# First product of two-slot expert units with the weights stationary, in a routed three-stage kernel

## Chip, cores and metric

One core of one Trainium2 chip runs the whole program. The metric is device microseconds of one launch; the median of three runs of the kernel before is 823.82 (823.65 to 824.0).

## What is computed

Attention over four batches of eight heads with window masks gives a matrix x of 2304 tokens by 512. Then come a feed-forward layer and a layer of eight experts in which each token goes to one expert:

```
h = x @ w_in                      # 512 x 2048
r = np.maximum(h, 0.0)
x = (s * (r * r) + b) @ w_out     # 2048 x 512
...
logits = xn @ en.T / tau          # both normalized, 8 experts
expert_idx = np.argmax(logits, axis=1)
gate_w = softmax(logits)[np.arange(N), expert_idx]
for e in range(E):
    mask = expert_idx == e
    h = np.maximum(x[mask] @ w1[e], 0.0)           # 512 x 1024
    out[mask] = gate_w[mask, None] * (h @ w2[e])   # 1024 x 512
```

## The kernel before

Every fp32 product is made of three products of a shorter type: each operand is split into a high part (a cast, on ACT) and a low part (what the cast left, a subtraction), and `mm3` (L271) adds high by high (L273), high by low (L274) and low by high (L275). The first operand is the stationary one (128 x 128, loaded by a weight load of its own), the second moves past it.

Attention and the feed-forward layer run first, interleaved. The tokens are sorted by expert into slots of 128. A unit is one or two slots of one expert. The first two slots (0, 1) belong to the most popular expert and are started early, while the feed-forward layer ends; the next two (2, 3) use the same weights, and then come a unit of two slots (4, 5) and five times a unit of one and a unit of two: 6; 7, 8; 9; 10, 11; and so on to 18; 19, 20. That is 21 slots, eight pairs and five singles; a tail for more slots stands in a branch that these inputs do not take.

For each unit `load` (L774) brings eight raw tiles of 512 KB by SP's queue, four of w1 and four of w2, and `split` (L789) makes the high parts on ACT (L802) and the low parts on DVE or, for one tile of four, on POOL (L803, L804). The parts go to one of two sets of buffers (`wp0`, `wp1`), which alternate by unit, so that a w1 tile of the unit after next can be split when this unit's first product has read it for the last time.

For each slot `gather` (L807) fetches 128 tokens by an indirect DMA of POOL. `xt` transposes them on PE into the bank px (four transposes, L818) and splits them into xh and xl. `g1` is the first product: the tokens are stationary, w1 moves, 48 matmuls of 512 columns in two halves, and ACT's relu gives h (L835). `ht` transposes h in eight blocks into two banks pt (L847) and splits them into hh and hl (L848, L849). `g2` is the second product, 24 matmuls of 512 columns with hh and hl stationary; DVE scales its rows by the gate into o (L860), and POOL scatters o by an indirect DMA (L861).

The banks px and pt, and those of the routing tables, come from one ring of three (`psT`, tag "tr"); `ph`, the first product's, from a ring of three, `po` from a ring of two. xh, xl, hh and hl have two buffers each, h has one, and the gathered tokens x have four.

PE runs in the order in which the program is written. The loop `slots` (L936) gives it: first product of slot j, transposes of the tokens of slot j + 1, second product of slot j - 1, transposes of h of slot j. The order on DVE, ACT, POOL and SP is set by the scheduler of the framework from the dependences, so one line of the program can stand far from its neighbour there. Ahead of the loop L911 to L934 write out the order of the first two slots, with the routing tables (`route_rest`, L675, `units`, L743, `slot_table`, L592) between them; DVE's arithmetic for the table and PE's matmuls into the bank ptabr (L611) give the gathers of all later slots.

Of the kernel before, what the change touches and what calls it, by code (L numbers as in the profile page):

```python
# [7 lines left out]
F32 = mybir.dt.float32  # L8
# [11 lines left out]
NTAIL = 7  # L20
# [27 lines left out]
class Kern:  # L48
# [740 lines left out]
    def split(self, j, after=None):  # L789
# [6 lines left out]
        for a in range(2):  # L796
            with ExitStack() as st:
                for ins in after[a] if after else ():
                    st.enter_context(self.tc.issue_after(ins.ins))
                for i in range(4):  # L800
                    h, l, r = w[8 * a + i], w[8 * a + 4 + i], self.raw[4 * a + i]
                    nc.scalar.copy(h, r)  # L802
                    eng = nc.gpsimd if i == 3 else nc.vector  # L803
                    eng.tensor_sub(l, r, h.bitcast(F32))  # L804
        return [w[4 * i:4 * i + 4] for i in range(4)]

    def gather(self, j, rows=NT):  # L807
        nc = self.nc
        x = self.xp.tile([P, DM], F32, tag="x", name=f"x{j}", bufs=4)
# [4 lines left out]
    def xt(self, j, x):  # L814
        nc = self.nc
        px = self.psT.tile([P, 512], F32, tag="tr", name=f"px{j}", bufs=3)
        for i in range(4):
            nc.tensor.transpose(px[:, P * i:P * i + P], x[:, P * i:P * i + P], self.ident)  # L818
        xh = self.xp.tile([P, DM], F32R, tag="xh", name=f"xh{j}", bufs=2)
        xl = self.xp.tile([P, DM], F32R, tag="xl", name=f"xl{j}", bufs=2)  # L820
        nc.scalar.copy(xh, px)
        self.last_xl = nc.vector.tensor_sub(xl, px, xh.bitcast(F32))
        return xh, xl

    def g1(self, j, xh, xl, w):
        nc = self.nc
        hs = self.pad.tile([P, EF], F32, tag="h", name=f"h{j}", bufs=1)

        def part(n):
            ph = self.psE.tile([P, 512], F32, tag="h", name=f"ph{j}_{n}", bufs=3)  # L830
            fs = slice(512 * n, 512 * n + 512)
            for k in range(4):
                ks = slice(P * k, P * k + P)
                self.mm3(ph, xh[:, ks], xl[:, ks], w[0][k][:, fs], w[1][k][:, fs], k == 0, k == 3)
            nc.scalar.activation(hs[:, fs], ph, AF.Relu)  # L835
        return hs, part

    def ht(self, j, hs):
        nc = self.nc
        hh = self.hp.tile([P, EF], F32R, tag="hh", name=f"hh{j}", bufs=2)  # L840
        hl = self.hp.tile([P, EF], F32R, tag="hl", name=f"hl{j}", bufs=2)
        for n in range(2):
            pt = self.psT.tile([P, 512], F32, tag="tr", name=f"pt{j}_{n}", bufs=3)
            fs = slice(512 * n, 512 * n + 512)
# [3 lines left out]
            nc.scalar.copy(hh[:, fs], pt)  # L848
            nc.vector.tensor_sub(hl[:, fs], pt, hh[:, fs].bitcast(F32))  # L849
        return hh, hl  # L850

    def g2(self, j, hh, hl, w):
        nc = self.nc
        po = self.psE.tile([P, 512], F32, tag="o", name=f"po{j}", bufs=2)
        for k in range(8):
            ks = slice(P * k, P * k + P)
            fs = slice(512 * (k % 2), 512 * (k % 2) + 512)
            self.mm3(po, hh[:, ks], hl[:, ks], w[2][k // 2][:, fs], w[3][k // 2][:, fs], k == 0, k == 7)
# [5 lines left out]
    def experts_early(self):  # L864
        self.gidx, self.sidx, self.gate, self.xs, self.xts = {}, {}, {}, {}, {}
# [15 lines left out]
    def experts_early3(self):  # L881
        self.xts[0] = self.xt(0, self.xs[0])
# [4 lines left out]
    def experts(self):  # L887
        nc, tc = self.nc, self.tc
        w, xs, xts, hts = self.w, self.xs, self.xts, {}
# [10 lines left out]
        first = {}  # L900
        for j, (u, _) in enumerate(slot):
            first.setdefault(u, j)
        n = len(slot)
        nstat = n - NTAIL
# [6 lines left out]
        hs0, part0 = self.g1(0, *xts.pop(0), w[0])  # L911
        part0(0)
        dots = self.logits_pe(NG - 1)
        part0(1)
        dots()
        tables = self.route_rest()
        xts[1] = self.xt(1, xs.pop(1))
        hts[0] = self.ht(0, hs0)
        hs1, part1 = self.g1(1, *xts.pop(1), w[0])
        part1(0)  # L920
        tables = tables()
        part1(1)
        hts[1] = self.ht(1, hs1)
        self.g2(0, *hts.pop(0), w[0])
# [3 lines left out]
        for j in range(2):  # L928
            xs[NEARLY + j] = self.gather(NEARLY + j)
        behind = [(self.last_gidx, self.last_gather)]  # L930
        load_for(1)
        self.g2(1, *hts.pop(1), w[0])
        xts[2] = self.xt(2, xs.pop(2))
        behind.append((self.last_xl,))  # L934

        def slots(j0, j1):  # L936
            for j in range(j0, j1 + 1):
                u = slot[j][0] if j < j1 else None
                ahead = j < j1 and (j == NEARLY or j == first[u]) and first.get(u + 1, j1) < j1
                if j < j1:  # L940
                    hs, part = self.g1(j, *xts.pop(j), w[u])
                    part(0)
                    part(1)
                if j == NEARLY:
# [5 lines left out]
                if j0 + 1 < j + 2 < j1:  # L950
                    xs[j + 2] = self.gather(j + 2)
                if ahead and u > 0:
                    load_for(u + 1)
                if j + 1 < j1:
                    xts[j + 1] = self.xt(j + 1, xs.pop(j + 1))
                if j > j0:
                    self.g2(j - 1, *hts.pop(j - 1), w[slot[j - 1][0]])
                if ahead:
                    w[u + 1] = self.split(u + 1, behind if j == NEARLY else None)
                if j < j1:  # L960
                    hts[j] = self.ht(j, hs)

        slots(NEARLY, nstat)
        used = nc.values_load(self.sexp[0:1, NUNIT:NUNIT + 1], min_val=0, max_val=2 * NPOS,  # L964
                              skip_runtime_bounds_check_because="a count of slots, made by comparisons")
        with tc.If(used > 2 * NPAIR + NSING):
            for i in range(2):
                xs[nstat + i] = self.gather(nstat + i)
            u = slot[nstat][0]
            load_for(u)  # L970
            w[u] = self.split(u)
            xts[nstat] = self.xt(nstat, xs.pop(nstat))
            slots(nstat, n)
# [60 lines left out]
```

## Time and profile before

| what | value |
|---|---|
| median of three runs | 823.82 us |
| the profiled execution | 825.07 us |
| its span, first to last instruction | 823.3 us |
| mean granted clock of PE | 0.984 of full |
| PE busy | 776.0 us |
| DVE busy | 563.6 us |
| ACT busy | 406.9 us |
| POOL busy | 184.1 us |

The profile is of one execution; its time stands 1.25 us above the median of the runs, and 1.77 above its own span. Busy times are averages over stages of different kind: attention and feed-forward layer take until about 560 us, the expert stage the rest. An engine's line in a timeline gives start, duration, source line, operation, result and operands, and in brackets the idle time before it with what ended it. A matmul's record is longer than its share of the engine, since matmuls overlap; the distance of two starts is the pace.

### The profile page before, as it was taken

What the parts mean: (1) busy time and instruction counts of PE and PEld (TensorE: products, weight loads), DVE (VectorE), ACT (ScalarE), POOL (GpSimd) and SP (SyncE); (2) the same over time, 40 slices, a digit from 0 to 9 for tenths busy, and PEclk for the clock granted to TensorE, in tenths of its full rate; (3) what the DMA queues carried; (4) which work ended last, traced back from release to release, by engine and by line L of the source; (5) the groups of instructions that cost most, each with busy time, mean ns of one, the idle gap of its engine ahead of it and who ended that gap; (6) DMA issues with size and microseconds to landing.
All of it is one profiled execution on the core that took longest, in us unless ns stands there. A gap on an engine that the chain in (4) does not pass through costs nothing. (4 is left out here: it accounts for less than half of the span.)

```text
span 823.3 us, 13887 instructions
## 1 busy us (share of the span) xinstructions
PE 776.0 (94%) x4898; PEld 664.5 (81%) x4898; DVE 563.6 (68%) x1339; ACT 406.9 (49%) x941; POOL 184.1 (22%) x131
## 2 busy tenths in 40 slices
PE   5678889999999999999999999897999999999996
PEld 4467777888888888888888998785788888888884
DVE  5888998877576647765776498858746665658431
ACT  5665664554355426442644323534456556657430
POOL 2564564000000000000000000302624544444320
PEclk9998999999999999999999999998999999999999
DMA  7555553221022103110300002311351159596300
GB/s 268 179 179 179 163 189 125 103 80 44 17 76 66 44 17 104 38 44 18 103 17 2 26 13 99 132 40 28 115 194 61 63 160 385 158 355 208 146 15 24
DMA packets 33373, 88.02 MB, mean 107 GB/s; under 512 B 4295, under 2 KB 4295, under 8 KB 33169
## 3 DMA queue, kind: packets, MB, share of 16 engines
q1 hardware_dynamic: 29936, 76.84, 27.8%
q0 software_dynamic: 3360, 10.23, 3.7%
q8 instruction: 41, 0.67, 0.3%
q14 instruction: 36, 0.29, 0.1%
HBM read 94.39 MB, written 10.22 MB: 127 GB/s over the span
## 5 line engine op out<-in xcount | busy, mean ns | idle before, releaser
L804 POOL TENSOR_TENSOR wl<-raw,wh 128x1024 fp32r<-128x1024 f32 x24 | 58.5, 2437 | 438.6 <-ACT wh L802 438.6
L275 PE MATMUL ph<-xhi,wil 128*128 128x384 f32 x384 | 131.4, 342 | 1.3 <-DVE wil L269 1.3
L273 PE MATMUL ph<-xhi,wih 128*128 128x384 f32 x384 | 132.0, 344 | 0.3 <-ACT wih L267 0.3
L274 PE MATMUL ph<-xlo,wih 128*128 128x384 f32 x384 | 131.2, 342 | 0.0
L804 DVE TENSOR_TENSOR wl<-raw,wh 128x1024 fp32r<-128x1024 f32 x72 | 99.5, 1417 | 38.2 <-ACT wh L802 38.1
L273 PE MATMUL py<-woh,gh 128*128 128x512 f32 x288 | 119.4, 415 | 0.1
L275 PE MATMUL py<-woh,gl 128*128 128x512 f32 x288 | 114.9, 399 | 2.3 <-DVE gl L289 2.3
L274 PE MATMUL py<-wol,gh 128*128 128x512 f32 x288 | 114.8, 399 | 0.0
L802 ACT CAST wh<-raw 128x1024 fp32r<-128x1024 f32 x96 | 97.2, 1047 | 20.8 <-PE po L275 11.6
L289 DVE SCALAR_TENSOR_TENSOR gl<-r,sb,gh 128x384 fp32r<-128x384 f32 x96 | 66.7, 695 | 51.8 <-ACT gh L288 49.5
L288 ACT ACTIVATE gh<-r,sb 128x384 fp32r<-128x384 f32 x96 | 58.9, 614 | 86.8 <-PE py L274 68.7
L284 ACT ACTIVATE r<-ph 128x384 f32<-128x384 f32 x96 | 46.7, 487 | 99.3 <-PE ph L275 99.2
L285 DVE SCALAR_TENSOR_TENSOR r<-r,sb 128x384 f32<-128x384 f32 x96 | 63.2, 658 | 35.9 <-ACT r L284 35.7
L507 DVE CUSTOM_DVE_ANT_0 junk<-ysb,enb 128x512 bf16<-128x512 f32 x120 | 82.4, 687 | 0.9
L273 PEld LDWEIGHTS ph<-xhi,wih 128*128 128x128 f32 x384 | 73.8, 192 | 4.9 <-ACT wih L267 0.8
L274 PEld LDWEIGHTS ph<-xlo,wih 128*128 128x128 f32 x384 | 73.6, 192 | 3.9
L275 PEld LDWEIGHTS ph<-xhi,wil 128*128 128x128 f32 x384 | 73.5, 192 | 1.6 <-DVE wil L269 1.6
L139 ACT ACTIVATE prob<-prob,st 128x80 f32<-128x80 f32 (+3 forms) x168 | 58.4, 349 | 29.9 <-DVE st L137 29.9
L273 PE MATMUL po<-wh,hh 128*128 128x512 f32 x168 | 69.0, 411 | 0.2 <-ACT hh L848 0.2
L273 PE MATMUL ph<-wh,xh 128*128 128x512 f32 x168 | 68.2, 406 | 0.7 <-issue 0.7
L275 PEld LDWEIGHTS py<-woh,gl 128*128 128x128 f32 x288 | 54.9, 191 | 16.2 <-DVE gl L289 3.2
L275 PE MATMUL po<-wh,hl 128*128 128x512 f32 x168 | 66.9, 398 | 0.0
(250 smaller groups left out, 1382.0 us busy)
## 6 DMA issues: line engine op xcount, KB each, us to landing
raw<-in_moe_w SPq DMA_DIRECT2D x96, 512.0 KB
raw<-in_moe_w_in SPq DMA_DIRECT2D x16, 512.0 KB
raw<-in_moe_w_out SPq DMA_DIRECT2D x16, 512.0 KB
qkd<-in_qkd SPq DMA_DIRECT2D x24, 288.0 KB
qkp<-in_qkp SPq DMA_DIRECT2D x12, 416.0 KB
ydram<-ysb SPq DMA_DIRECT2D x18, 256.0 KB
vd<-in_vd SPq DMA_DIRECT2D x24, 160.0 KB
vp<-in_vp SPq DMA_DIRECT2D x12, 288.0 KB
```

The source lines that it names most:

```text
L139: nc.scalar.activation(prb[:, t, :w], prb[:, t, :w], AF.Exp, scale=-1.0, bias=st[:, t:t + 1], accum_out=st[:, 4 + t:5 + t])
L273: nc.tensor.matmul(out, lhsT=ah, rhs=bh, start=first, stop=False)
L274: nc.tensor.matmul(out, lhsT=ah, rhs=bl, start=False, stop=False)
L275: nc.tensor.matmul(out, lhsT=al, rhs=bh, start=False, stop=last)
L284: nc.scalar.activation(r, ph[:, :G], AF.Relu)
L285: nc.vector.scalar_tensor_tensor(out=r, in0=r, scalar=self.sb[:, 0:1], in1=r, op0=ALU.mult, op1=ALU.mult)
L288: nc.scalar.activation(gh, r, AF.Identity, bias=self.sb[:, 1:2])
L289: nc.vector.scalar_tensor_tensor(out=gl, in0=r, scalar=self.sb[:, 1:2], in1=gh.bitcast(F32), op0=ALU.add, op1=ALU.subtract)
L507: ins = nc.vector.tensor_tensor_reduce(out=self.junk, in0=y, in1=self.enb[:, e], scale=1.0, scalar=0.0, op0=ALU.mult, op1=ALU.add, accum_o ...
L802: nc.scalar.copy(h, r)
L804: eng.tensor_sub(l, r, h.bitcast(F32))
```

## The change

A unit of two slots gets a first product of its own, `g1_pair`: a 128 x 128 block of w1 is stationary, and the 256 tokens of both slots move. Its result is the hidden values already transposed, so that pairs have no `ht`. A pair has four quarters of 24 matmuls of 256 columns; for each, ACT writes relu into hh, and DVE takes the maximum with zero and subtracts hh in one operation. Units of one slot keep `g1` and `ht`. `xt` now takes both slots of a unit, into halves of one tile. xh, xl, hh and hl have one buffer, of the size of a pair, and x has five. All subtractions of `split` are DVE's. The transposed tokens of the logits (`logits_pe`) use two tiles of the weight buffers. The loop goes by units: first product of unit r, transposes of h if it is a single, transposes of the tokens of unit r + 1, second product of its first slot, and for a pair the first product of the next single ahead of the second slot's second product.

```diff
 def logits_pe(self, g):
-        yT = [self.hp.tile([P, EF], F32, tag=t, name=f"yT{t}", bufs=2) for t in ("hh", "hl")]
+        yT = [self.wp1.tile([P, EF], F32, tag=t, name=f"yT{t}") for t in ("wl12", "wl13")]
...
 def split(self, j, after=None):
                     nc.scalar.copy(h, r)
-                    eng = nc.gpsimd if i == 3 else nc.vector
-                    eng.tensor_sub(l, r, h.bitcast(F32))
+                    nc.vector.tensor_sub(l, r, h.bitcast(F32))
...
 def gather(self, j, rows=NT):
-        x = self.xp.tile([P, DM], F32, tag="x", name=f"x{j}", bufs=4)
+        x = self.xp.tile([P, DM], F32, tag="x", name=f"x{j}", bufs=5)
...
+    def xt(self, js, xs):
+        nc, w = self.nc, P * len(js)
+        xh = self.xp.tile([P, 4, w], F32R, tag="xh", name=f"xh{js[0]}")
+        xl = self.xp.tile([P, 4, w], F32R, tag="xl", name=f"xl{js[0]}")
+        for n, (j, x) in enumerate(zip(js, xs)):
+            px = self.psT.tile([P, 512], F32, tag="tr", name=f"px{j}", bufs=3)
+            for i in range(4):
+                nc.tensor.transpose(px[:, P * i:P * i + P], x[:, P * i:P * i + P], self.ident)
+            p3 = px.rearrange("p (k t) -> p k t", k=4)
+            h, l = (y[:, :, P * n:P * n + P] for y in (xh, xl))
+            nc.scalar.copy(h, p3)
+            self.last_xl = nc.vector.tensor_sub(l, p3, h.bitcast(F32))
+        return xh, xl
...
+    def g1_pair(self, js, xh, xl, w):
+        nc = self.nc
+        hh, hl = self.hidden(js)
+        def part(n):
+            ph = self.psE.tile([P, 2, 256], F32, tag="h", name=f"ph{js[0]}_{n}", bufs=3)
+            for i in range(2):
+                fs = slice(P * (2 * n + i), P * (2 * n + i) + P)
+                for k in range(4):
+                    self.mm3(ph[:, i], w[0][k][:, fs], w[1][k][:, fs], xh[:, k], xl[:, k], k == 0, k == 3)
+            ns = slice(2 * n, 2 * n + 2)
+            nc.scalar.activation(hh[:, ns], ph, AF.Relu)
+            nc.vector.scalar_tensor_tensor(out=hl[:, ns], in0=ph, scalar=0.0, in1=hh[:, ns].bitcast(F32),
+                                           op0=ALU.max, op1=ALU.subtract)
+        return (hh, hl), part
...
 def experts_early3(self):
-        self.xts[0] = self.xt(0, self.xs[0])
+        self.xt0 = self.xt([0, 1], [self.xs.pop(0), self.xs.pop(1)])
...
+        hts, part = self.g1_pair([0, 1], *self.xt0, w[0])
+        part(0)
         dots = self.logits_pe(NG - 1)
+        part(1)
         dots()
         tables = self.route_rest()
+        part(2)
         tables = tables()
+        part(3)
+        self.g2(0, 0, *hts, w[0])
         gi, rest = tables()
...
+        def go(r0, r1):
+            for r in range(r0, r1):
+                js, more = runs[r], r + 1 < r1
+                if len(js) == 2:
+                    hts, part = self.g1_pair(js, *xts.pop(r), w[r])
+                    for i in range(4):
+                        part(i)
+                elif r not in hs:
+                    single(r)
...
+                if r + 2 < r1:
+                    gather(r + 2)
+                if more and r > 0:
+                    load_for(r + 1)
+                if len(js) == 1:
+                    hts = self.ht(js[0], hs.pop(r))
+                if more:
+                    xt(r + 1)
+                self.g2(js[0], 0, *hts, w[r])
+                if more:
+                    w[r + 1] = self.split(r + 1, behind if r == 0 else None)
+                if len(js) == 2:
+                    if more and len(runs[r + 1]) == 1:
+                        single(r + 1)
+                    self.g2(js[1], 1, *hts, w[r])
```

Three places show how the instructions move. In a name the first number after the letters is the slot (xl7, hl6, o5) or, for wh and wl, the matrix (0 for w1, 1 for w2), the tile and, after the underscore, the unit; px and pt are banks of the ring of three.

**DVE, from the end of the unit of slots 4 and 5 through the one-slot unit of slot 6.** Before:

```order
L804 TENSOR_TENSOR wl00_4_6843<-raw0_5458,wh00_4_6842 128x1024
L804 TENSOR_TENSOR wl01_4_6845<-raw1_5459,wh01_4_6844 128x1024
L804 TENSOR_TENSOR wl02_4_6847<-raw2_5460,wh02_4_6846 128x1024
L822 TENSOR_TENSOR xl7_6680<-px7_6674,xh7_6679 128x512
L804 TENSOR_TENSOR wl10_3_6722<-raw4_5462,wh10_3_6721 128x1024
L804 TENSOR_TENSOR wl11_3_6724<-raw5_5463,wh11_3_6723 128x1024
L860 TENSOR_SCALAR o5_6708<-po5_6683,gater_6270 128x512
L804 TENSOR_TENSOR wl12_3_6726<-raw6_5464,wh12_3_6725 128x1024
L849 TENSOR_TENSOR hl6_6746<-pt6_0_6747,hh6_6745 128x512
L849 TENSOR_TENSOR hl6_6746<-pt6_1_6754,hh6_6745 128x512
```

After:

```order
L803 TENSOR_TENSOR wl00_4_7019<-raw0_5458,wh00_4_7018 128x1024
L803 TENSOR_TENSOR wl01_4_7021<-raw1_5459,wh01_4_7020 128x1024
L803 TENSOR_TENSOR wl02_4_7023<-raw2_5460,wh02_4_7022 128x1024
L803 TENSOR_TENSOR wl03_4_7025<-raw3_5461,wh03_4_7024 128x1024
L803 TENSOR_TENSOR wl10_3_6831<-raw4_5462,wh10_3_6830 128x1024
L803 TENSOR_TENSOR wl11_3_6833<-raw5_5463,wh11_3_6832 128x1024
L881 TENSOR_SCALAR o5_6742<-po5_6717,gater_6380 128x512
L803 TENSOR_TENSOR wl12_3_6835<-raw6_5464,wh12_3_6834 128x1024
L803 TENSOR_TENSOR wl13_3_6837<-raw7_5465,wh13_3_6836 128x1024
L870 TENSOR_TENSOR hl6_6761<-pt6_0_6762,hh6_6760 128x512
L870 TENSOR_TENSOR hl6_6761<-pt6_1_6769,hh6_6760 128x512
L825 TENSOR_TENSOR xl7_6777<-px7_6778,xh7_6776 128x4x128
```

The subtraction of the fourth tile of w1 and of w2 has come from POOL, and both stand ahead of the low part of slot 6's hidden values. The low part of slot 7's tokens, which stood ahead of w2's, now stands behind everything.

**PE, at the end of slot 5's second product, with the semaphores that an instruction waits for.** Before:

```order
L847 MATMUL pt6_0_6747<-ident_60,h6_6632 128x128 [waits Activation_49]
L847 MATMUL pt6_0_6747<-ident_60,h6_6632 128x128 x3
L847 MATMUL pt6_1_6754<-ident_60,h6_6632 128x128 [waits Activation_49]
L847 MATMUL pt6_1_6754<-ident_60,h6_6632 128x128 x3
L273 MATMUL ph7_0_6762<-wh00_3_6713,xh7_6679 128x512 [waits Activation_49]
L274 MATMUL ph7_0_6762<-wl00_3_6714,xh7_6679 128x512
L275 MATMUL ph7_0_6762<-wh00_3_6713,xl7_6680 128x512 [waits DVE_49]
...
L275 MATMUL ph7_1_6776<-wh03_3_6719,xl7_6680 128x512
L818 MATMUL px8_6803<-ident_60,x8_6661 128x128 [waits DMASW2_49,PE_49]
L818 MATMUL px8_6803<-ident_60,x8_6661 128x128 x3
L273 MATMUL po6_6812<-wh10_2_6506,hh6_6745 128x512 [waits Activation_49]
```

After:

```order
L275 MATMUL po5_6717<-wh13_1_6444,hl4_6493 128x512
L866 MATMUL pt6_0_6762<-ident_60,h6_6688 128x128 [waits Activation_49]
L866 MATMUL pt6_0_6762<-ident_60,h6_6688 128x128 x3
L866 MATMUL pt6_1_6769<-ident_60,h6_6688 128x128 [waits Activation_49]
L866 MATMUL pt6_1_6769<-ident_60,h6_6688 128x128 x3
L821 MATMUL px7_6778<-ident_60,x7_6602 128x128 [waits DMASW1_49,PE_49]
L821 MATMUL px7_6778<-ident_60,x7_6602 128x128 x3
L821 MATMUL px8_6785<-ident_60,x8_6604 128x128 [waits DMASW2_49,DVE_49]
L821 MATMUL px8_6785<-ident_60,x8_6604 128x128 x3
L273 MATMUL po6_6792<-wh10_2_6664,hh6_6760 128x512 [waits Activation_49]
```

Before, the transposes of slot 6's hidden values are followed by slot 7's first product, and px8 waits for a DMA and for PE. Now both px follow at once, and px8, the fourth bank in a row from a ring of three, waits for DVE.

**ACT, in the unit of slots 4 and 5.** Before:

```order
L835 ACTIVATE h5_6546<-ph5_0_6547 128x512
L802 CAST wh00_3_6713<-raw0_5458 128x1024
L802 CAST wh01_3_6715<-raw1_5459 128x1024
L802 CAST wh02_3_6717<-raw2_5460 128x1024
L835 ACTIVATE h5_6546<-ph5_1_6561 128x512
L802 CAST wh03_3_6719<-raw3_5461 128x1024
L821 CAST xh6_6582<-px6_6577 128x512
```

After:

```order
L843 ACTIVATE hh4_6492<-ph4_1_6521 128x512
L843 ACTIVATE hh4_6492<-ph4_2_6548 128x512
L802 CAST wh00_3_6822<-raw0_5458 128x1024
L802 CAST wh01_3_6824<-raw1_5459 128x1024
L802 CAST wh02_3_6826<-raw2_5460 128x1024
L802 CAST wh03_3_6828<-raw3_5461 128x1024
L843 ACTIVATE hh4_6492<-ph4_3_6575 128x512
L824 CAST xh6_6617<-px6_6619 128x512
```

The four casts of w1 for unit 3 stood around a relu of slot 5. Now all four stand ahead of the relu of the pair's last quarter (ph4_3).

## Rows read from the trace of the kernel before

**Rows 1.** Page, busy time (us), share of the span and instructions of PE.
```profile
PE 776.0 (94%) x4898; PEld 664.5 (81%) x4898; DVE 563.6 (68%) x1339; ACT 406.9 (49%) x941; POOL 184.1 (22%) x131
```

**Rows 2.** Windows, expert stage: start:end, length, busy (x instructions) per engine, PEclk, DMA share, GB/s.
```profile
604.70:641.97 37.27, 37.27 (x182) 30.69 (x180) 24.72 (x24) 23.70 (x31) 17.13 (x10) 1.00 0.29 94
...
679.24:716.50 37.26, 37.26 (x181) 30.69 (x180) 24.77 (x24) 23.71 (x31) 17.17 (x10) 1.00 0.74 267
...
753.77:791.03 37.26, 37.26 (x181) 30.70 (x180) 18.86 (x21) 20.23 (x27) 10.21 (x6) 1.00 0.44 166
```

**Rows 3.** Waits of PE, 560 to 823: us in total, times, longest.
```profile
PE ptabr L611 <- DVE btr L606: 4.6, 1, 4.6
```

**Rows 4.** Timeline of PE in the FFN: widths 512 and 384.
```profile
300.40 0.40 PE L273 MATMUL py<-woh,gh 128*128 128x512 f32 x1
...
302.48 0.34 PE L273 MATMUL ph<-xhi,wih 128*128 128x384 f32 x1
...
304.57 0.40 PE L273 MATMUL py<-woh,gh 128*128 128x512 f32 x1
```

**Rows 5.** Timeline of PE, one-slot unit: start, us, engine, line, operation.
```profile
635.51 1.03 PE L847 MATMUL pt<-ident,h 128*128 128x128 f32 x8
...
636.62 0.39 PE L274 MATMUL ph<-wl,xh 128*128 128x512 f32 x1
```

**Rows 6.** Timeline of the weight loads (PEld), expert stage.
```profile
629.90 0.19 PEld L273 LDWEIGHTS po<-wh,hh 128*128 128x128 f32 x1
630.01 0.19 PEld L274 LDWEIGHTS po<-wl,hh 128*128 128x128 f32 x1
```

**Rows 7.** Page, costliest groups: busy, mean ns; idle before, releaser.
```profile
L804 POOL TENSOR_TENSOR wl<-raw,wh 128x1024 fp32r<-128x1024 f32 x24 | 58.5, 2437 | 438.6 <-ACT wh L802 438.6
```

**Rows 8.** Timeline of DVE, around the one-slot unit.
```profile
628.77 3.50 DVE L804 TENSOR_TENSOR wl<-raw,wh 128x1024 fp32r<-128x1024 f32 x3 [3.10 <-ACT wh L802]
...
636.69 0.74 DVE L860 TENSOR_SCALAR o<-po,gater 128x512 f32<-128x512 f32 x1
...
637.36 2.96 DVE L804 TENSOR_TENSOR wl<-raw,wh 128x1024 fp32r<-128x1024 f32 x1
...
640.24 1.27 DVE L849 TENSOR_TENSOR hl<-pt,hh 128x512 fp32r<-128x512 f32 x2
```

**Rows 9.** Timeline of ACT, with the PE row ahead of its relu.
```profile
627.69 2.95 ACT L802 CAST wh<-raw 128x1024 fp32r<-128x1024 f32 x3
...
803.31 0.39 PE L275 MATMUL ph<-wh,xl 128*128 128x512 f32 x1
...
803.74 0.60 ACT L835 ACTIVATE h<-ph 128x512 f32<-128x512 f32 x1 [2.14 <-PE ph L275]
```

**Rows 10.** Timeline of DVE, routing table.
```profile
560.64 0.31 DVE L759 TENSOR_TENSOR unite<-unite,unit 128x152 f32<-128x152 f32 x1
...
561.88 0.18 DVE L766 CAST sexp<-se 128x20 int32<-128x20 f32 x1
```

**Rows 11.** Timeline of PE, end of the kernel.
```profile
808.99 1.03 PE L847 MATMUL pt<-ident,h 128*128 128x128 f32 x8
...
811.33 0.40 PE L273 MATMUL po<-wh,hh 128*128 128x512 f32 x1
```

**Rows 12.** Windows with the clock: columns as in rows 2.
```profile
100.20:102.10 1.90, 0.00 (x1) 0.00 (x0) 1.90 (x8) 0.76 (x2) 0.69 (x1) 1.00 0.29 30
103.50:106.80 3.30, 3.30 (x11) 2.72 (x10) 3.30 (x5) 2.26 (x7) 2.27 (x2) 0.50 0.23 48
525.60:527.60 2.00, 0.00 (x0) 0.00 (x0) 2.00 (x4) 0.00 (x0) 1.67 (x2) 1.00 0.00 0
527.70:531.00 3.30, 3.30 (x17) 3.00 (x18) 1.88 (x5) 1.61 (x3) 1.87 (x2) 1.00 0.39 97
562.70:567.20 4.50, 0.00 (x0) 0.00 (x0) 4.43 (x18) 4.28 (x5) 1.02 (x1) 1.00 0.15 58
567.70:574.40 6.70, 6.70 (x24) 5.10 (x22) 6.35 (x16) 2.89 (x4) 2.78 (x2) 0.50 0.09 15
```

More of the change, by code (lines that the diff above doesn't have):

```diff
@@ L812, in gather, with hidden @@
         return x
-    def xt(self, j, x):
-        nc = self.nc
[L816 to L823, printed above, removed]
+    def xt(self, js, xs):
[11 more added lines that the diff above has]
+        return xh, xl
+    def hidden(self, js):
+        return [self.hp.tile([P, 8, P * len(js)], F32R, tag=t, name=f"{t}{js[0]}") for t in ("hh", "hl")]
+    def g1_pair(self, js, xh, xl, w):
+        nc = self.nc
+        hh, hl = self.hidden(js)
[10 more added lines that the diff above has]
+        return (hh, hl), part
     def g1(self, j, xh, xl, w):
@@ L827, in g1 @@
         hs = self.pad.tile([P, EF], F32, tag="h", name=f"h{j}", bufs=1)
-        def part(n):
+        for n in range(2):
             ph = self.psE.tile([P, 512], F32, tag="h", name=f"ph{j}_{n}", bufs=3)
@@ L888, in experts @@
         nc, tc = self.nc, self.tc
-        w, xs, xts, hts = self.w, self.xs, self.xts, {}
+        w, xs, xts, hs = self.w, self.xs, {}, {}
         order = [1]
@@ L899, in experts @@
         slot = [(u, p) for u, ps in enumerate(units) for p in ps]
-        first = {}
-        for j, (u, _) in enumerate(slot):
-            first.setdefault(u, j)
         n = len(slot)
-        nstat = n - NTAIL
+        runs = [[j for j in range(NEARLY, n) if slot[j][0] == u] for u in range(len(units))]
+        nstat = len(runs) - NTAIL
         ecur = {0: self.em}
@@ L927, in experts, with gather, xt, single @@
             self.gidx[j] = gi[:, slot[j][1]:slot[j][1] + 1]
-        for j in range(2):
-            xs[NEARLY + j] = self.gather(NEARLY + j)
+        def gather(r):
+            for j in runs[r]:
+                xs[j] = self.gather(j)
+        def xt(r):
+            xts[r] = self.xt(runs[r], [xs.pop(j) for j in runs[r]])
+        gather(0)
         behind = [(self.last_gidx, self.last_gather)]
         load_for(1)
-        self.g2(1, *hts.pop(1), w[0])
-        xts[2] = self.xt(2, xs.pop(2))
+        self.g2(1, 1, *hts, w[0])
+        xt(0)
         behind.append((self.last_xl,))
[L936 to L944, printed above, removed]
+        gather(1)
+        def single(r):
+            hs[r] = self.g1(runs[r][0], *xts.pop(r), w[r])
+        def go(r0, r1):
[7 more added lines that the diff above has]
+                    single(r)
+                if r == 0:
                     self.gates_late()
@@ L949, in slots @@
                         self.sidx[i], self.gate[i] = si[:, p:p + 1], ga[:, p:p + 1]
[L950 to L963, printed above, removed]
+                if r + 2 < r1:
[13 more added lines that the diff above has]
+                    self.g2(js[1], 1, *hts, w[r])
+        go(0, nstat)
         used = nc.values_load(self.sexp[0:1, NUNIT:NUNIT + 1], min_val=0, max_val=2 * NPOS,
@@ L966, in experts @@
         with tc.If(used > 2 * NPAIR + NSING):
[L967 to L973, printed above, removed]
+            gather(nstat)
+            gather(nstat + 1)
+            load_for(nstat)
+            w[nstat] = self.split(nstat)
+            xt(nstat)
+            go(nstat, len(runs))
 _INS = ["qkp", "qkd", "vp", "vd", "moe_w_in", "moe_w_out", "moe_s", "moe_b", "moe2_expert_emb", "moe2_tau", "moe2_w1", "moe2_w2"]
```

33 lines of the change are left out of this document (11 added, 22 removed).

## The prediction, made before the changed kernel was run

> **What bounds the kernel now.** I read the page first, for the engine that is busiest [rows 1]: PE works 776 us, 94% of the span, so only a look at the stages says where another engine matters. The windows come next. The run of five equal stretches from 604.70 to 791.03 (three are shown) is the steady part of the expert stage, each one one-slot unit and one two-slot unit [rows 2]: PE is busy for all 37.27 us of each, at the full clock, while DVE has 24.7 us of work and POOL 17. The list of waits says the same from the other side: in the last 260 us PE waits once for long, 4.6 us for the routing table, and otherwise under 1 us [rows 3]. So in this stage time is the sum of PE's instructions, and a shorter list saves time as long as no other engine becomes late.
>
> The two sizes that make up the 37.27 come from PE's timeline. Nine matmuls of 512 columns fill 300.40 to 302.48, 0.231 each; twelve of 384 fill 302.48 to 304.57, 0.174 each [rows 4]. From 635.51 to 636.62 there are eight transposes and one matmul [rows 5]: (1.11 - 0.231) / 8 = 0.110 for a transpose. Three slots with 12 transposes and 48 matmuls each give 36 x 0.110 + 144 x 0.231 = 37.2, the window.
>
> **The change part by part.** *Transposes.* Sixteen slots lose the eight transposes of their hidden values: 128 x 0.110 = **-14.1 us** on PE, all of it on the path.
>
> *Matmuls of half the width.* The eight pairs have 768 matmuls of 256 columns for 384 of 512. A straight line through 384 and 512 [rows 4] gives 0.231 - 2 x 0.057 = 0.117 for 256, which over 768 is 1.3 us more than half of 0.231 each; strict proportion gives nothing. The risk is the load of the stationary tile, which now has to be over in half the time. The recorded loads last 0.19, but two stand 0.11 apart, 629.90 and 630.01 [rows 6], so they overlap, and a load fits behind a matmul of 0.117. Bounds: 0, and, if a load of 0.19 sets the pace, 768 x (0.19 - 0.117) = +56. I take **0**, by the spacing that the rows show.
>
> *Subtractions from POOL to DVE.* 24 of 96 weight subtractions, 2.44 us each on POOL [rows 7], now run on DVE. DVE's own take 1.17 with POOL quiet (3.50 for 3) and up to 2.96 beside one on POOL [rows 8]. Over a stretch DVE has room; what counts is when DVE is due, and the orders above show two places.
>
> First, **the one-slot unit**. PE's ring of three banks for transposes now sees pt, pt, px, px in a row, and the second px takes the bank of the first pt: it waits for DVE's hl of the first half. In DVE's order four w1 subtractions of the unit after next, two of w2, the other slot's o and two more of w2 stand ahead of that hl. Count from the start of the second half of the single's first product. PE: 12 matmuls 2.78, the other slot's second product 24 x 0.231 to 8.34, eight transposes to 9.21, the first px to 9.65; there it wants the second px. ACT: the buffer of the first w1 tile comes free with the third matmul, which starts at 0.46; from a matmul's start to ACT's is 0.43 (803.31, 803.74), and from the first cast to the first subtraction 1.08 (627.69, 628.77) [rows 8, 9]. DVE therefore starts at about 1.98; 6 x 1.17 to 8.98, o 0.67 (636.69 to 637.36) to 9.65, 2 x 1.17 to 11.98, hl 0.64 (1.27 for 2) [rows 8] to 12.62. ACT's nine casts and relus, 0.97 each at most, stay ahead of it. From an end to PE's next start I take 0.43 - 0.23 = 0.20. PE stands for 12.62 + 0.20 - 9.65 = 3.2 us, at four singles. At the fifth no w1 subtractions follow; o waits for the other slot's product (8.34 + 0.20), then 0.67 + 2.33 + 0.64 + 0.20, a stand of 2.7. Together **+15.4**. Bounds: nothing, if DVE gains 3.2 us; above, if DVE meets its slow subtractions (2.96), but POOL has none left. The old rows show the same lateness with a cover: there hl ran at 640.24 although the transposes started at 635.51 [rows 5, 8], some 4 us late, and PE had 24 matmuls of the next slot in between. That cover is what the change takes away.
>
> Second, **the last quarter of a pair**. ACT's order has four w1 casts ahead of the last relu, DVE's the four subtractions ahead of the last max-and-subtract. From the start of that quarter: first w1 tile free after 15 matmuls of 0.116 plus 0.20 = 1.94, first subtraction 3.02, four to 7.68, the last operation 0.64 (nearest row: hl, same width out of PSUM) plus 0.20 to 8.52. PE: 2.78, one px 0.44, and the second product's 21st matmul, the first to read that quarter's low part, 20 x 0.231 on, at 7.84. A stand of 0.67, five times: **+3.3**. Bounds 0 and twice that.
>
> *Start of the stage.* In DVE's order o of slot 0 now stands ahead of the rest of the table arithmetic, which ran from 560.64 to 562.06 under PE's second product [rows 10]: 1.4 us more in front of the 4.6 us wait [rows 3]. The first pair also needs both halves of its tokens split, one more operation of 0.6 [rows 9]. **+2.0**, between 0 and 3.
>
> *End.* The last slot's transposes, cast and wait go from 808.99 to 811.33, 2.34 us [rows 11], of which 8 x 0.110 and three matmuls are counted already or remain: 2.34 - 0.88 - 0.69 = **-0.8**.
>
> *Token gathers, loads, scatters.* The weight loads on SP keep their order and wait for the same casts; DMA is busy 0.74 of a stretch at most [rows 2]; a gather is now asked for two units ahead, with five buffers for it. POOL, without subtractions, comes to its gathers and scatters sooner. Nothing, covered by a whole unit of PE's work (12 to 25 us).
>
> *The clock.* The granted clock has two levels, 2.4 GHz and half of it. In rows 12 PE stood 1.9 us (100.20 to 102.10) and the clock was 0.50 of full in the 3.3 us from 103.50; it stood 4.5 us (562.70 to 567.20) and 6.7 us at 0.50 followed. But after 2.0 us (525.60 to 527.60) it stayed 1.00. A stand of 3.2 lies between the case of 1.9 and that of 4.5, both of which were punished: I take 3.3 us at half speed, 1.7 lost, after each of the four long stands, and none after the 2.7 or the 0.67: **+6.8**. Bounds: 0, and 3.35 (half of 6.7) after all five, +16.8.
>
> A rule speaks against the change here. The Trainium skill, "TensorE: Matmul & The Clock Gate", section "Part 4: PE-mode transpose", says that transposes do not count as work for the clock as matmuls do. By that rule the twelve transposes on either side of the stand belong to the quiet time, and the fifth stand is followed by a slow stretch too; no row here separates transposes from matmuls, so the trace neither agrees nor differs.
>
> **Sum**: -14.1 + 0 + 15.4 + 3.3 + 2.0 - 0.8 + 6.8 = +12.6. The profiled execution took 825.07, of which 823.3 is the span; the median is 823.82. Against its own time that is 837.7, and with the 1.25 between them taken off, **836.4**.
>
> **The rivals.**
> - *The stands come, the clock stays.* For it: 2.0 us at 525.60 without a fall. Against: 1.9 us at 100.20 with one [rows 12]. Sum without 6.8: +5.8, **829.6**, 0.15.
> - *Clock falls after all five stands*, 1.7 each, as in the forecast but with the transposes beside the stand as quiet time too: +8.5 for 6.8, **838.1**, 0.13. This is what the rule of the Trainium skill named above would make of it.
> - *It falls for longer*, as after 562.70: 5 x 3.35 = 16.8 for 6.8, **846.4**, 0.09.
> - *The other side: DVE is not late.* If DVE works off the nine operations ahead of hl 3.2 us sooner than reckoned, the second px finds its bank free; then the quarter's 0.67 goes too and no clock falls. -14.1 + 2.0 - 0.8 = -12.9: **810.9**, 0.14. For it: DVE is 24.7 of 37.27 us busy [rows 2], and all its subtractions now run without POOL beside them. Against: they are counted at 1.17 already, and start only when PE lets go of the w1 tiles. It decides where DVE's hl of the first half ends before PE ends the first px.
> - *In between*: stands of 1.9 us, 5 x 1.9 = 9.5 for 15.4, no clock loss: -0.1, **823.7**, no change, 0.06.
> - *The change doesn't do what it says*: matmuls of 256 columns don't take half the time, because the loads set the pace. 1 ns more on each is 0.8 us; at 0.19, 836.4 + 56. Against: loads 0.11 apart [rows 6]. 0.05.
>
> **How the numbers follow.** My forecast has the remaining 0.38. A measurement of this kernel can tell 0.2%, 1.65 us, from no change. Faster: 0.14 of the other side and 0.01 from the edge of the case in between, 0.15; same 0.06; slower 0.79. The range leaves out the other side (0.14) and the slow loads (0.05): from the case in between less its edge, 822, to the longer fall plus 1.5 for the second stand at its upper bound, 848.
>
> **What would show it.** Right: no transposes of hidden values in pairs; 96 matmuls of a pair's first product in 11.1 to 11.3 us; PE's waits name the second px behind DVE's hl, some 3 us five times, and the second product behind the last max-and-subtract under 1 us; a 0.50 stretch behind the stands. Wrong: no wait of px, then the time is near 811; a first product well over 11.3 us; or a wait for gathers, weight loads or ACT, for which nothing is counted here.

## The result, and the profile of the changed kernel

The changed kernel takes 835.84 us (median of four runs, 832.46 to 837.11) against 823.91 for the kernel before on the same chip: a ratio of 1.0134, 95% interval 1.0117 to 1.0152. The forecast was 836.4, slower, in a range of 822 to 848. The profiled execution took 836.87, its span is 835.1; the span of before was 823.3, so 11.8 us are to be found.

The page first. PE has less to do than before [rows 1], yet the span is longer. DVE has all 96 weight subtractions, at 1.22 us each where POOL took 2.44 [rows 7].

```profile
span 835.1 us, 14314 instructions
...
PE 772.5 (92%) x5154; PEld 677.1 (81%) x5154; DVE 571.3 (68%) x1363; ACT 391.0 (47%) x909; POOL 131.2 (16%) x107
...
L803 DVE TENSOR_TENSOR wl<-raw,wh 128x1024 fp32r<-128x1024 f32 x96 | 113.0, 1221 | 45.5 <-ACT wh L802 45.2
```

The waits of PE from 555 us to the end (in total, times, longest) answer to [rows 3], which was a single long wait. Now five stops behind hl add 13.1 us, the wait for the table has grown by 1.4, and there is a wait for gathered tokens.

```profile
PE px L821 <- DVE hl L870: 13.1, 5, 2.7
PE ptabr L611 <- DVE btr L606: 6.1, 1, 6.1
PE px L821 <- DMA x<-ydram,gidxr: 1.9, 1, 1.9
PE po L275 <- DVE hl L844: 1.1, 5, 0.2
```

The place is the one-slot unit. On PE's timeline the transposes pt and the first px run as forecast, and the second px stands for 2.73 us; the same place comes again 40.69 us later (633.94, 674.63), where the stretches of before took 37.27 [rows 2].

```profile
633.94 1.03 PE L866 MATMUL pt<-ident,h 128*128 128x128 f32 x8
634.81 0.60 PE L821 MATMUL px<-ident,x 128*128 128x128 f32 x4
638.14 0.85 PE L821 MATMUL px<-ident,x 128*128 128x128 f32 x4 [2.73 <-DVE hl L870]
...
674.63 1.03 PE L866 MATMUL pt<-ident,h 128*128 128x128 f32 x8
```

DVE's timeline over the same stretch shows what hl stood behind: six weight subtractions without a gap, the other slot's o, two more subtractions, then hl at 637.40. Its first half ends about 638.0 and PE goes on at 638.14.

```profile
627.65 6.90 DVE L803 TENSOR_TENSOR wl<-raw,wh 128x1024 fp32r<-128x1024 f32 x6 [3.81 <-ACT wh L802]
634.47 0.75 DVE L881 TENSOR_SCALAR o<-po,gater 128x512 f32<-128x512 f32 x1
635.14 2.35 DVE L803 TENSOR_TENSOR wl<-raw,wh 128x1024 fp32r<-128x1024 f32 x2
637.40 1.28 DVE L870 TENSOR_TENSOR hl<-pt,hh 128x512 fp32r<-128x512 f32 x2
```

The clock is read from windows of the same trace (columns as in rows 2, the clock third from the end). Behind each of the four stops of 2.7 us there is a stretch at or near 0.50 (a mean a little above it where the window reaches past one of its ends); behind the fifth, of 2.13 us, there is none. Two more half-speed stretches stand where the kernel before has none: one at 546, where PE had not stopped at all, and one at 578, behind the wait for tokens.

```profile
546.50:549.30 2.80, 2.80 (x15) 2.80 (x14) 2.35 (x14) 0.22 (x1) 0.00 (x0) 0.50 0.00 0
578.00:583.80 5.80, 5.66 (x25) 5.36 (x26) 5.13 (x5) 0.00 (x0) 4.21 (x3) 0.50 0.49 153
638.70:641.40 2.70, 2.70 (x9) 2.11 (x8) 1.28 (x2) 0.59 (x1) 1.94 (x2) 0.50 0.60 197
679.20:682.20 3.00, 3.00 (x10) 2.34 (x9) 1.47 (x3) 0.76 (x2) 1.99 (x2) 0.54 0.92 284
719.80:722.80 3.00, 3.00 (x12) 2.41 (x11) 1.54 (x3) 0.93 (x2) 1.99 (x2) 0.60 1.09 346
760.50:763.50 3.00, 3.00 (x13) 2.41 (x10) 1.51 (x3) 1.20 (x2) 0.00 (x0) 0.64 0.98 320
801.00:804.50 3.50, 3.50 (x17) 2.81 (x16) 1.06 (x2) 0.51 (x1) 0.00 (x0) 1.00 0.19 71
```

On PE's timeline the routing's matmuls of 8 columns stand ahead of the stretch at 546:

```profile
543.64 2.74 PE L534 MATMUL pd<-enT,yTwl 128*128 128x8 f32 x24
```

Last, the pace of the matmuls of 256 columns on PE's timeline. From 607.72 to 616.48 there are 74 of them: 0.1184 each, 11.37 us for a pair's 96. (In the kernel before a slot's first product is 24 matmuls of 512 columns, not the 48 given in its description; 48 are two slots'.)

```profile
607.72 0.28 PE L274 MATMUL ph<-xl,wh 128*128 128x256 f32 x1
...
616.48 0.60 PE L821 MATMUL px<-ident,x 128*128 128x128 f32 x4
```

### The profile page after: what moved, and what is told of

Read it like the earlier page. It is cut to its first block, busy times and chain, and to the rows that moved or that the text cites. A ratio compares the mean times of both kernels' runs of the same rounds, so it can differ in the third digit from the quotient of the medians.

```text
span 835.1 us, 14314 instructions
## 1 busy us (share of the span) xinstructions
PE 772.5 (92%) x5154; PEld 677.1 (81%) x5154; DVE 571.3 (68%) x1363; ACT 391.0 (47%) x909; POOL 131.2 (16%) x107
## 5 line engine op out<-in xcount | busy, mean ns | idle before, releaser
L803 DVE TENSOR_TENSOR wl<-raw,wh 128x1024 fp32r<-128x1024 f32 x96 | 113.0, 1221 | 45.5 <-ACT wh L802 45.2
L273 PE MATMUL ph<-xh,wh 128*128 128x256 f32 x256 | 74.2, 290 | 0.7 <-issue 0.7
L274 PE MATMUL ph<-xl,wh 128*128 128x256 f32 x256 | 73.9, 289 | 0.1
L275 PE MATMUL ph<-xh,wl 128*128 128x256 f32 x256 | 73.7, 288 | 0.0
L275 PE MATMUL po<-wh,hl 128*128 128x512 f32 x168 | 69.1, 411 | 1.1 <-DVE hl L844 1.1
```

What stands on the lines that cost most here:

```text
L273: nc.tensor.matmul(out, lhsT=ah, rhs=bh, start=first, stop=False)
L274: nc.tensor.matmul(out, lhsT=ah, rhs=bl, start=False, stop=False)
L275: nc.tensor.matmul(out, lhsT=al, rhs=bh, start=False, stop=last)
L803: nc.vector.tensor_sub(l, r, h.bitcast(F32))
```

## The experiments

The theory: DVE's queue makes the stops, and each long stop also costs clock. Against it: the ring of three banks or PE's own order makes them; or taking the subtractions from POOL does. Ratios are to the kernel before, run beside each.

| run | what | median us | ratio, 95% interval |
|---|---|---|---|
| e1 | hl ahead of half of w2 | 819.72 | 0.9938, 0.9915 to 0.9960 |
| e2 | hl ahead of a quarter of w2 | 825.26 | 1.0008, 0.9995 to 1.0021 |
| e3 | second px inside the product | 833.72 | 1.0105, 1.0081 to 1.0130 |
| e4 | POOL's subtractions back | 841.99 | 1.0205, 1.0183 to 1.0227 |
| e5 | before, with DVE's subtractions alone | 821.50 | 0.9969, 0.9956 to 0.9981 |
| e6 | e1, o of slot 0 behind the table | 814.38 | 0.9866, 0.9846 to 0.9886 |
| e7 | e1, four buffers of tokens | 816.67 | 0.9911, 0.9888 to 0.9934 |
| e8 | e6 and e7, px inside the product | 811.81 | 0.9862, 0.9845 to 0.9878 |
| e9 | e8, small matmuls mixed in | 811.65 | 0.9856, 0.9838 to 0.9874 |

**e1: hl first.** The split of the next unit's third and fourth w2 tile is ordered behind the single's hh and hl.

```diff
+                    if late is not None and a == 1 and i == 2:
+                        for ins in late:
+                            st.enter_context(self.tc.issue_after(ins.ins))
                     nc.scalar.copy(h, r)
                     nc.vector.tensor_sub(l, r, h.bitcast(F32))
...
-                    w[r + 1] = self.split(r + 1, behind if r == 0 else None)
+                    w[r + 1] = self.split(r + 1, behind if r == 0 else None, (self.last_hh, self.last_hl) if len(js) == 1 else None)
```

> The changed kernel, but at a one-slot unit the third and fourth tile of the next unit's w2 are split (cast and subtraction) behind the slot's hidden values hh and hl, not ahead of them. Theory (DVE's queue makes the stop): in the trace of the change DVE is done with six weight subtractions and the o ahead of hl at 635.14, and ACT's cast of hh waits behind another weight cast to 635.09. With both out of the way hh is cast from about 634.5, hl ends about 635.7, and the second px, wanted at 635.25, stops for 0.5 to 0.8 instead of 2.73; five stops of 3 to 4 us together for 13.1. Short stops leave the clock at full: no half-speed stretches behind them, another 6.8. Together 835.8 - 9.5 - 6.8 = 819 to 820. Rival (the ring of three banks or the order of PE itself makes the stop, whatever stands ahead of hl): the stops stay at 2.7 and the time at 834 to 837. Second rival (the clock falls with the quiet of the twelve transposes alone): 826 with stops gone and the half-speed stretches still there.

Measured 819.72. DVE's timeline in e1 has hl right behind o, and the two subtractions behind it:

```profile
626.78 6.90 DVE L806 TENSOR_TENSOR wl<-raw,wh 128x1024 fp32r<-128x1024 f32 x6 [3.81 <-ACT wh L805]
633.59 0.75 DVE L884 TENSOR_SCALAR o<-po,gater 128x512 f32<-128x512 f32 x1
634.32 1.29 DVE L873 TENSOR_TENSOR hl<-pt,hh 128x512 fp32r<-128x512 f32 x2
635.75 2.36 DVE L806 TENSOR_TENSOR wl<-raw,wh 128x1024 fp32r<-128x1024 f32 x2
```

In the list of PE's waits px stands for 0.5 us at most, and in windows of 2 us from 590 on the clock is full until PE has ended:

```profile
PE px L824 <- DVE hl L873: 2.6, 5, 0.5
```

On PE's timeline the same place comes again after 36.91 us, 40.69 in the change:

```profile
633.07 1.03 PE L869 MATMUL pt<-ident,h 128*128 128x128 f32 x8
...
669.98 1.03 PE L869 MATMUL pt<-ident,h 128*128 128x128 f32 x8
```

The ring of three banks and PE's order are the same as in the change; only what stands ahead of hl differs. So the order on DVE and ACT made the stops, and the stops made the slow clock; the transposes beside them are the same in both, and without a long stop no slow stretch follows. Of the 3.78 us between the two distances 2.20 are the shorter stop (2.73 to 0.53), so a half-speed stretch cost about 1.6. Of the 16.1 us in all, 10.5 are stops (13.1 less 2.6), and the other 5.6 are near the 6.3 of four such stretches.

**e2: half of the way.** Only the fourth w2 tile's split stands behind hl, on DVE alone (i == 3 for i == 2 in the diff above, and hl without hh).

> The changed kernel, with only the fourth tile of w2 behind hl on DVE: one subtraction of 1.17 us fewer ahead of it. Both theory and rivals of the stop give 2.73 - 1.17 = 1.6 us at four singles and about 1.0 at the fifth, 7.3 in all for 13.1: 830 if the clock falls as before. The run tells the clock apart: if what counts is how long PE stands, 1.6 us is shorter than the 1.9 that was followed by half speed and than the 2.13 of the fifth stop, which was not, so no half-speed stretches and 835.8 - 5.8 - 6.8 = 823; if the transposes around the stop count as quiet too, the clock falls as before and the time is 830.

Measured 825.26, between the two cases; ten runs spread from 822.73 to 826.09. In PE's waits the stops are as reckoned, 1.6 us and 7.4 in all:

```profile
PE px L823 <- DVE hl L872: 7.4, 5, 1.6
```

In the profiled execution (822.73) no half-speed stretch follows a stop; the window behind the first shows it:

```profile
634.50:637.00 2.50, 2.47 (x13) 2.11 (x14) 2.50 (x4) 0.97 (x2) 2.19 (x2) 1.00 0.35 105
```

Its mean granted clock is 0.982; in six of the other nine executions, 825 to 826 us, it is 0.977. That fits about two half-speed stretches more, but where they stood in those executions was not seen. They need not be behind the stops: the change has a stretch at 546, which the profiled execution of e2 lacks, and at 578 a longer one (577.0 to 583.9) than e2 (576.5 to 579.9). So stops of 1.6 us cost no clock in the execution that shows them; whether they did in the others stays open.

**e3: px moved on PE.** The second px stands inside the single's second product, behind its fifth group of three matmuls (`mid` is its transposes, cast and subtraction).

```diff
+            if mid is not None and k == 5:
+                mid()
             self.mm3(po, hh[:, k, ts], hl[:, k, ts], w[2][k // 2][:, fs], w[3][k // 2][:, fs], k == 0, k == 7)
```

> The changed kernel, with the transposes of the second slot's tokens moved on PE from ahead of the single's second product into it, behind its fifth of eight groups of three matmuls. If the ring of three banks is the cause, the second px no longer has a bank to wait for, the stops vanish and with them the half-speed stretches: about 816. If DVE's lateness is the cause, the stop only moves to the third matmul of the second product, which reads the same hl: it wants it at about 635.7, gets it at 638.1, stops of 2.3 us named po behind hl and not px, 835.8 - 2 = 834 with the clock falling, 827 if 2.3 us leave the clock at full as the fifth stop of 2.13 did.

Measured 833.72. The bank's wait is gone from the list of PE's waits, and the stop stands at the product's third matmul instead, behind the same hl. The ring was where the lateness showed, not its cause.

```profile
PE po L275 <- DVE hl L880: 7.8, 5, 1.7
```

PE's timeline at the first of the five:

```profile
636.85 0.50 PE L273 MATMUL po<-wh,hh 128*128 128x512 f32 x1 [0.31 <-ACT hh L879]
...
639.25 0.69 PE L275 MATMUL po<-wh,hl 128*128 128x512 f32 x1 [1.66 <-DVE hl L880]
```

The stop is 1.7 at four singles and 1.1 at the fifth, and not 2.3, partly because PE now waits for ACT's hh at the first matmul already. The clock fell behind three of the four stops of 1.7 in this execution. Where it fell, the distance from one single to the next is 40.28 us for 40.69 in the change (635.07 to 675.35), so most of the loss stayed.

**e4: POOL back.** `eng = nc.gpsimd if i == 3 else nc.vector` as before, all else as in the change.

> The changed kernel, with the subtraction of every fourth weight tile back on POOL; all else as in the change. Theory (DVE subtractions beside POOL's take up to 2.96 instead of 1.17, so that moving them cost DVE nothing): hl comes as late as in the kernel before, 640.89 for 636.82 there, so stops of about 4 us, 20 for 13.1, the clock falls behind all five: 843 to 848, slower than the change. Rival (taking the subtractions from POOL is what made DVE late): two subtractions fewer ahead of hl, stops of 0.4, no half-speed stretches, 816 to 820.

Measured 841.99, 6.2 above the change and 1 us short of the theory's range. One subtraction of DVE beside POOL's takes 2.70, and hl starts at 640.80, with stops of 4.2 at four singles and 1.1 at the fifth, 17.8 in all; the clock fell at each of the four. Not all of the 6.2 comes from there: the first px starts at 534.50 (531.18 in the change), since the wait that e5 is about is back ahead of it, 2.09 us, and in this execution the clock fell there too (527.0 to 530.4). DVE's timeline in e4:

```profile
637.52 0.74 DVE L882 TENSOR_SCALAR o<-po,gater 128x512 f32<-128x512 f32 x1
638.18 2.70 DVE L804 TENSOR_TENSOR wl<-raw,wh 128x1024 fp32r<-128x1024 f32 x1
640.80 1.28 DVE L871 TENSOR_TENSOR hl<-pt,hh 128x512 fp32r<-128x512 f32 x2
```

POOL's, at the same time:

```profile
637.23 2.57 POOL L804 TENSOR_TENSOR wl<-raw,wh 128x1024 fp32r<-128x1024 f32 x1 [1.85 <-ACT wh L802]
```

So taking the subtractions from POOL was the good part of the change, not what made DVE late.

**e5: that part alone**, put into the kernel before (the same one line).

> The kernel before, with one part of the change alone: every subtraction of the weights on DVE, none on POOL. In the kernel before hl was some 4 us late at a one-slot unit, but 24 matmuls of the next slot covered it, so in the expert stage PE keeps its 37.27 us per stretch and nothing is won there. What the part can win lies ahead of it: the wait of py behind DVE's gl at 525.60 was 2.0 us in the kernel before and is 0.6 to 1.2 in kernels without POOL's subtractions. Theory: 1 to 3 us less, 821 to 823. Rival (the POOL part is where the change loses, whatever the order of the rest): slower than before, by the 28 us of added DVE work as far as it is not hidden, 826 or more.

Measured 821.50, 0.3% faster than before. What can be traced of the gain lies ahead of the expert stage. In the trace of before a DVE operation of 128 x 2 elements lasts 2.33 us while POOL subtracts, gl comes late behind it, and PE stands for 2.10. The timelines of the kernel before there, DVE first:

```profile
524.70 2.33 DVE L618 TENSOR_SCALAR gidxe<-tke 128x2 uint32<-128x2 f32 x1
...
527.01 0.60 DVE L289 SCALAR_TENSOR_TENSOR gl<-r,sb,gh 128x384 fp32r<-128x384 f32 x1
```

POOL:

```profile
524.53 2.46 POOL L804 TENSOR_TENSOR wl<-raw,wh 128x1024 fp32r<-128x1024 f32 x1 [4.54 <-ACT wh L802]
```

PE, which waits for gl:

```profile
527.67 0.50 PE L275 MATMUL py<-woh,gl 128*128 128x512 f32 x1 [2.10 <-DVE gl L289]
```

In e5 the same operation of DVE takes 0.15, and the wait is 0.6 (in the changed kernel 0.54):

```profile
522.75 0.15 DVE L618 TENSOR_SCALAR gidxe<-tke 128x2 uint32<-128x2 f32 x1
```

That is 1.5 of the 2.8 us. The rest isn't traced: in the profiled executions e5 is 1.5 us ahead at 165 us already, long before POOL's first weight subtraction at 516.9.

**e6: o behind the table.** The product of slot 0 leaves its bank as it is, and o is made behind the slots' indices.

```diff
-        self.g2(0, 0, *hts, w[0])
+        po0 = self.g2(0, 0, *hts, w[0], defer=True)
         gi, rest = tables()
+        with tc.issue_after(self.last_gidx.ins):
+            self.g2_out(0, po0)
```

> As e1, and o of slot 0 stands behind the routing table's arithmetic on DVE, not in the middle of it. If o's place is what made the wait for the table grow from 4.65 to 6.07, the wait falls back to 4.6 to 4.8, everything behind it comes 1.4 us sooner, 818.3. Rival (the gathers of the first pair set the pace behind the table, so that the wait only moves to the tokens): the table comes sooner, the wait for the gathered tokens is longer by as much, 819.7.

Measured 814.38, 4 us better than the theory's figure. The wait for the table is 4.6 again, and the wait for tokens, which the rival wanted to grow, is gone. The gathers tell why. In e1 POOL issues the first two beside DVE's weight subtractions, 1.79 and 1.94 us. POOL's timeline, then DVE's:

```profile
569.82 1.79 POOL L812 DMA_INDIRECT x<-ydram,gidxr  x1 [8.02 <-DVE emr L622]
571.91 1.94 POOL L812 DMA_INDIRECT x<-ydram,gidxr  x1 [0.30 <-issue]
```

```profile
569.54 3.49 DVE L806 TENSOR_TENSOR wl<-raw,wh 128x1024 fp32r<-128x1024 f32 x3
```

In e6 o stands between the indices and those subtractions, and the first two issues take 0.95 and 1.17, 1.6 us less together, more than the 1.4 that PE waited for tokens in e1:

```profile
567.43 0.95 POOL L812 DMA_INDIRECT x<-ydram,gidxr  x1 [40.74 <-DVE gidxr L618]
568.68 1.17 POOL L812 DMA_INDIRECT x<-ydram,gidxr  x1 [0.30 <-issue]
```

```profile
567.07 0.74 DVE L890 TENSOR_SCALAR o<-po,gatee 128x512 f32<-128x512 f32 x1
...
567.81 4.62 DVE L806 TENSOR_TENSOR wl<-raw,wh 128x1024 fp32r<-128x1024 f32 x4
```

The second issue lies beside the subtractions as well and is short, and a third beside them (570.16) takes 1.96. So the shorter issues are measured; that the subtractions alone make the long ones isn't shown.

With the tokens there in time the second half-speed stretch, behind their wait (at 578 to 581 in e1's trace), is not there either.

**e7: four buffers of tokens** (`bufs=4` in `gather`), on e1.

> As e1, with four buffers of gathered tokens and not five. Theory (a gather is asked for two units ahead and three slots' tokens are waiting at most once the loop runs): no difference in the loop, 819 to 820.5. Rival (the fifth buffer is needed): PE waits for gathered tokens at units of two slots, some 2 us each as at the first pair, and the time goes above 824.

Measured 816.67. The fifth buffer is not needed: from one single to the next the loop takes 36.92 us (629.72 to 666.64), as in e1. That four are quicker isn't shown, since the intervals of e1 and e7 overlap and the two profiles differ ahead of the expert stage and in where the clock fell.

**e8: the rest of the stop.** e6 and e7 together, with the second px behind the second group of the product (k == 2 in e3's diff).

> As e6, with four buffers of gathered tokens, and the transposes of the second slot's tokens moved on PE behind the second of eight groups of the single's second product. The short stops left in e1 and e6 (0.5 us, five times, the second px behind hl) are the time of a cast and a subtraction behind the transposes; with px further back PE has two matmuls to do before it needs hl, so 0.5 becomes 0.1 or so: 2 us less than e6, 812 to 813. Rival (the stop only moves to the product's third matmul, as in e3): 814.

Measured 811.81, 1.4% faster than before. px no longer stands among PE's waits, and the stop didn't move to the product: now that hl comes early, the kind of edit that in e3 only moved the stop removes what was left. On PE's timeline one single follows the other after 36.53 us, 36.91 in e6 (628.24 to 665.15):

```profile
626.97 1.03 PE L879 MATMUL pt<-ident,h 128*128 128x128 f32 x8
...
663.50 1.03 PE L879 MATMUL pt<-ident,h 128*128 128x128 f32 x8
```

Five times 0.4 is 2 of the 2.6 us below e6. The other 0.6 isn't told apart: the profile of e8 has no half-speed stretch at 546, that of e6 has one.

**e9: small matmuls mixed in.** The routing's 24 matmuls of 8 columns stand in three groups inside the second quarter of the early pair's first product.

```diff
                     self.mm3(ph[:, i], w[0][k][:, fs], w[1][k][:, fs], xh[:, k], xl[:, k], k == 0, k == 3)
+                    if mix is not None and (i, k) in ((0, 3), (1, 1)):
+                        mix(i)
```

> As e8, with the routing's matmuls of 8 columns, which stand as one block of 24 (2.6 us, PE busy all the while) behind the second quarter of the early pair's first product, mixed into that quarter in three groups; they end at the same time. In most traces of the changed structure the granted clock is at half for some 3.3 us behind that block although PE never stood. If small matmuls count as little work for the clock, the half-speed stretch about 546 goes in most executions: up to 1.7 us less, 811 to 812, and no window at 0.50 between 540 and 556. If that stretch has another cause (the start of the stage, transposes of the tokens before it) it stays, and the time is that of e8.

Measured 811.65, the same as e8, and inconclusive: its profile has no half-speed window about 546, but e8's, with the block whole, has none either.

## Why the prediction was right, and where its sum was luck

The answer and the mechanism held: PE stands behind hl at the five one-slot units. The terms, from the profiled executions of before and of the change:

| term | forecast | measured |
|---|---|---|
| 128 transposes | -14.1 | -13.9 (0.87 for eight, 633.94 to 634.81) |
| matmuls of 256 columns | 0 | +2.2 (0.1184 for 0.1155, 768 times) |
| stops at singles | +15.4 | +13.1 |
| last quarter of a pair | +3.3 | +1.1 |
| table | +1.4 | +1.4 (6.07 for 4.65) |
| split of the first pair's second half | +0.6 | 0 (PE's 0.67 ahead of that product stands in both) |
| gathers | 0 | +1.9 (the wait for the first pair's tokens) |
| clock behind the stops | +6.8 | +6.3 (four stretches, 1.6 each by e1) |
| clock elsewhere | 0 | some +3 (estimates from PE's pace there: 1.5 at 546, 2.6 at 578, 1.1 less behind the table) |
| ahead of the expert stage | 0 | -2.4 (the early tokens' px at 531.18 for 533.57; 1.6 of it is the wait behind gl, the rest is there at 165 us already) |
| end | -0.8 | -0.8 (slot 20's second product follows slot 19's without a wait) |

The measured column adds to 11.9, and the spans differ by 11.8; the parts of the clock are estimates, so that the sum is closer than its terms are known. Point by point:

- **The one-slot unit** was read right from rows of before: DVE's subtractions start 2.0 us behind the start of the second half of the single's first product (625.68, 627.65), and o follows them. The stop of 3.2 was 2.73: DVE reached hl 0.26 sooner than reckoned, PE the second px 0.08 later, and from DVE's end to PE's start it took 0.1, not 0.20. The fifth was 2.13 for 2.7: one subtraction stood behind o there, not two.
- **The clock** fell behind four stops and not the fifth, as forecast, but partly by luck. The forecast let a stand of 2.7 go free and charged stands of 3.2; the stops that were followed by half speed were of 2.73. A fifth stop of 2.7, as it was forecast, would by these four have cost clock too.
- **The last quarter of a pair** was sized at 0.67 and is 0.2 in the list of waits: DVE ended its four subtractions 0.2 sooner than reckoned, and from DVE's end to PE's start it took 0.06, not 0.20.
- **Matmuls of half the width**: the straight line gave +1.3 and proportion nothing; the pace of 0.1184 makes it 2.2, and a pair's 96 took 11.37 us, just outside the 11.1 to 11.3 that was to show the forecast right. The loads didn't set a pace of 0.19.
- **"Nothing, covered by a whole unit of PE's work"** for the gathers failed at the first pair, which has no unit ahead of it to cover them: 1.9 us, and a half-speed stretch behind it that no term had. The prediction had named a wait for gathers as a sign of being wrong.
- **POOL's subtractions** were priced in the expert stage alone. Their removal also frees DVE ahead of it: 1.5 us of the gain of e5.

So the hit of 0.6 us between 836.4 and 835.84 is partly two kinds of error that cancel, which is luck: the stops, the quarters, the split, the clock behind the stops and the front came out 8.0 lower than forecast, and matmuls, gathers, transposes and the clock elsewhere about 7.3 higher. Of the rivals, "DVE is not late" would have given 810.9; e8, in which DVE's order has been mended, lands at 811.81, with the start of the stage mended as well.

The clock's rival drew on the Trainium skill, "TensorE: Matmul & The Clock Gate", section "Part 4: PE-mode transpose", by which a transpose doesn't count as busy time in the way that a matmul does. By that rule the transposes beside the stop would be quiet time as well, and the fifth stop would be followed by a slow stretch. The trace of the change has four stretches, not five, and in e1 none follows the same transposes, which speaks against that outcome in these executions; the rule itself was not put to a test of its own.

## What to carry to other kernels

When PE is busy all the time, an operation that comes late on another engine costs nothing until the matmuls that covered it are taken away: before removing PE work, list what each remaining PE instruction waits for and what is queued ahead of that on its engine. If it is late, put the operation that PE wants ahead of work that is wanted a unit later; here two edges in DVE's and ACT's order were worth 16 us, more than the 13.9 us of transposes that the change itself removed. Moving the waiting instruction on PE mostly moves the wait as long as its producer is late (e3); once the producer was early it removed the 0.5 us that was left (e8).

## What the runs showed of the hardware

- An operation on DVE of 256 elements took 2.33 us while POOL subtracted (before, e4) and 0.15 to 0.17 in the kernels whose POOL doesn't. One weight subtraction of DVE took 2.70 beside POOL's (e4), and 1.22 on average without it (the change).
- Gathers issued by POOL behind the table took between 0.94 and 1.96 us in e6. The long ones lay beside DVE's subtractions, but so did short ones (1.17, 0.98); what makes an issue long stays open.
- Stops of nearly the same length are not treated alike by the clock: 2.73 us was followed by half speed four times of four, 2.13 was not, 1.7 (e3) three times of four, 1.6 (e2) never in the execution that was profiled. The wait of py behind gl was 2.1 us in the kernel before and in e4, and half speed came with it in e4 alone. What beside the length decides it stays open.
- The granted clock fell in the changed kernel at 546 behind 24 matmuls of 8 columns, with PE busy all the while. It fell behind the same block in e1, e3, e4 and e6, and in e5, whose order on PE is that of the kernel before; it didn't there in the kernel before, e2, e7 and e8. So the block alone doesn't decide it, and e9 didn't settle what does.
